# Taking the transposed queries from 16 rows of 128 tokens each, with an exp that reads PSUM in permuted order

## The chip, the cores and the metric

The kernel runs on one core of one Trainium2 chip. The core's engines work side by side and wait for each other through semaphores: PE (TensorE, the matmuls), DVE (VectorE), ACT (ScalarE), POOL (GpSimd) and SP (SyncE, which here only issues transfers). The metric is the device time of one execution in microseconds; lower is better. Profiles are of one execution, and in them "us" are counted from the first instruction.

## The reference

Two steps follow each other, in float32. First, attention with pooled keys: for each of four batches, 12288 queries `q` of 128 channels attend to 768 keys, which are 4 x 4 means of `kv` (384 x 32 positions) times a weight matrix; the values are the same as the keys. Then a mixture of adapters: each of the 49152 result rows picks two of eight experts, and a low-rank correction is added.

```
kv_pool = kv.reshape(B, H // r, r, W // r, r, C).mean(axis=(2, 4))      # r = 4
k = v = kv_pool.reshape(B, -1, C) @ w_sr
a = softmax(q @ k^T / sqrt(C));  x = (a @ v).reshape(B * S, D)
logits = x @ w_gate                         # 8 experts, top 2, weights by softmax of the two
out = x + sum over the two experts e of  w_e * ((x @ A[e]) @ B[e])
```

The output has 49152 rows of 128 floats.

## The kernel before, in words

The tokens are taken in 96 *chunks* of T = 512, and four chunks make a *group* of GT = 2048 (24 groups in all). In a group the kernel is free to choose which token stands in which column, as long as the exp's output, the attention rows and the stores agree.

**How queries reach PE.** PE needs q transposed, channels on partitions. For groups 0 and 1, `load_q` loads q in float32 and `turn_q` transposes it on PE in four parts, with a copy on ACT (L116). For groups 2 to 23, `cast_q` writes a bf16 copy to DRAM with a POOL-issued transfer, and `load_qT` (L84) reads it with one transposing DMA on SP's queue. Before the change that DMA reads the group as 128 rows of 16 tokens: row p, token j is token 16p + j of the group, and it lands in column 128j + p of `qT`. A chunk is a quarter of these columns. The transpose of a group is issued at the first chunk of the group before it; `qT` has four buffers.

**One chunk.** `scores` runs three times (r = 0, 1, 2). Each time PE writes two 128-key blocks of scores into a PSUM tile `sg` of 128 x 2 x 512 floats (two buffers), and ACT's exp (L246) turns the 1024 floats of each partition into fp16 `em`. Then `attend` takes 128-column pieces of `em`, one for each s = 0 to 3, as the stationary operand, so that partition p of the result `acc` belongs to column 128s + p of the chunk. `normalize`, `top`, `route`, `gates`, `transposes`, `down`, `gate` and `up` do the softmax division and the adapters on DVE, POOL, ACT and PE. `finish` (L363, L364) adds the correction on DVE and stores the chunk from SP: partition p holds four consecutive tokens, so each of the 128 runs is 2 KB. The output tiles `osb` have six buffers.

**The order of the work.** It is written out by hand: every call is wrapped in `keep`, which keeps program order on its engine. The main loop runs over chunks k, with the score matmuls of chunk k between the attend matmuls of an earlier one and the adapter work of still earlier ones. While a batch runs, the keys of the next batch are loaded (L96, on SP) and summed on POOL (L171).

**The start.** Before all that, the weights are loaded from ACT's queue, and on SP's queue come group 0's queries (L105, one transfer of 1 MB), 24 transfers of 256 KB with the first batch's `kv` (L98), and group 1's queries in four transfers. The first batch's keys are summed on DVE and PE, part by part as they land.

Of the kernel before, what the change touches and what calls it, by code (L numbers as in the profile page):

```python
# [14 lines left out]
AF = mybir.ActivationFunctionType  # L15
# [5 lines left out]
def kernel(  # L21
# [10 lines left out]
    nc = tc.nc  # L32
    P = 128
# [6 lines left out]
    S = T // P  # L40
    GC = 4
    GT = GC * T
# [4 lines left out]
    scale = 1.0 / float(np.sqrt(C))  # L47
# [17 lines left out]
    keep = tc.keep_in_program_order  # L65

    def mm(*a, **k):
        return keep(nc.tensor.matmul(*a, **k))  # L68
# [6 lines left out]
    q_bf, qT, kvr = {}, {}, {}  # L75
# [5 lines left out]

    def load_qT(g):
        t = qpool.tile([P, GT], BF16, tag="qT", name="qT")
        keep(nc.sync.dma_start(t.rearrange("c (j p) -> c j p", p=P),  # L84
                               q_bf[g].rearrange("(p j) c -> p (j c)", p=P), transpose=True))
        qT[g] = t


# [9 lines left out]
            keep(nc.sync.dma_start(kvr[b, h][:, r, x], src[:, :, x * 4 * C:(x + 1) * 4 * C]))  # L98


    def load_q(g, lo, hi):
        if g not in q_f:
            q_f[g] = xpool.tile([P, GT // P, C], FP32, tag="xn", name="qf")
        src = q[0, g * GT:(g + 1) * GT].rearrange("(p j) c -> p j c", p=P)
        keep(nc.sync.dma_start(q_f[g][:, lo:hi], src[:, lo:hi]))  # L105

    def turn_q(g, m, engine):
        if m == 0:
# [11 lines left out]
    q_f = {}  # L120
    w_sr_sb = const.tile([P, C], FP32)
    keep(nc.scalar.dma_start(w_sr_sb, w_sr))
    w_gate_sb = const.tile([P, E], FP32)
    keep(nc.scalar.dma_start(w_gate_sb, moe_w_gate))
    load_q(0, 0, GC * S)
    for h in range(3):
        for r in range(4):
            for x in range(2):
                load_kv(0, h, r, x)
    for m in range(GC):  # L130
        load_q(1, m * S, m * S + S)
# [102 lines left out]
    em, acc, xn, xg, srt, gw = {}, {}, {}, {}, {}, {}  # L234
# [3 lines left out]
    def scores(k, r):  # L238
        b = k // NB
        if r == 0:  # L240
            em[k] = ppool.tile([P, J, T], FP16, tag="em", name="em")
        rhs = qT[k // GC][:, (k % GC) * T:(k % GC + 1) * T]
        ps = ps_s.tile([P, 2, T], FP32, tag="sg", name="sg")
        for i in range(2):
            mm(ps[:, i], kfT[b][:, 2 * r + i], rhs, start=True, stop=True)
        keep(nc.scalar.activation(em[k][:, 2 * r:2 * r + 2], ps, AF.Exp, bias=0.0, scale=scale))  # L246

    def attend(k, s):
        b = k // NB
# [111 lines left out]
    def finish(k):  # L361
        osb = opool.tile([P, S, C], FP32, tag="osb", name="osb")
        keep(nc.vector.tensor_tensor(osb, dp[k], xn[k][:, :, 0:C], op=ALU.add))  # L363
        keep(nc.sync.dma_start(  # L364
            out[k // GC * GT:(k // GC + 1) * GT].rearrange("(p j) c -> p j c", p=P)
            [:, k % GC * S:(k % GC + 1) * S], osb))
        for d in (em, acc, xn, xT, hgT, hp, hg, dp):
            d.pop(k, None)

# [5 lines left out]
    for h in range(3):  # L375
        for item in sums[h]:
            item()
        rest[3 * h]()
        if h > 0:
            scores(2, h - 1)  # L380
        rest[3 * h + 1]()
        if h > 0:
            scores(3, h - 1)
            rest[3 * h - 1]()
        scores(0, h)
        scores(1, h)
# [35 lines left out]
    for k in range(LA, last + 3):  # L422
        b, i = divmod(k, NB)
# [3 lines left out]
        if k % GC == 0:  # L427
            g = k // GC
            if 2 <= g + 1 < B * NG:
                load_qT(g + 1)  # L430
            if 4 <= g + 2 < B * NG and g + 2 not in q_bf:
                cast_q(g + 2)
        if b + 1 < B:
            if i == 4:
                sums, rest = prepare(b + 1, nc.gpsimd)
            if 4 <= i < 16:
                h, j = divmod(i - 4, 4)
# [28 lines left out]
        for u_ in ku:  # L466
            up(u_)
            finish(u_)
# [25 lines left out]
        if not ks:  # L494
            for u_ in ku:
                up(u_)
                finish(u_)
            ku = []
        kh = kx
        if b + 1 < B and 8 <= i < 20:  # L500
            h, j = divmod(i - 8, 4)
# [33 lines left out]
```

The softmax here doesn't subtract the row's maximum and nothing guards it: scores larger than these inputs give would overflow.

## Time and profile before

| | |
|---|---|
| median of 9 runs | 426.51 us (425.78 to 426.8) |
| the profiled execution | 426.8 us, with a span of 424.8 us from its first to its last instruction |
| busy share of PE / DVE / ACT / POOL | 91% / 77% / 69% / 38% |
| exp, L246 | 288 instructions, 1023 ns each |
| transposing DMA, L84 | 22 on SP's queue, median 8.1 us from issue to landing |
| stores, L364 | 96 of 256 KB, median 3.3 us to landing |
| DMA packets | 71172, of them 49904 under 512 B |
| granted TensorE clock | 0.975 of full speed on average |

An engine's busy time is the sum of its instructions' durations. Rows of groups give the line, engine, operation, output <- input, the count, then busy time and mean of one, then the idle time of the engine just before them and who ended it. Rows of waits read "engine, line <- who was waited for: us in total, times, longest". Timeline rows give the start and the length in us; several instructions in a row on one engine are merged, with their count behind the x. "SPq" is SP's queue while it issues a transfer.

### The profile page before, as it was taken

Reading aid. Unit: us, or ns where it says so; the run is one execution under the profiler, and the core shown is the slowest. Engines: PE = TensorE matmul, PEld = TensorE weight load, DVE = VectorE, ACT = ScalarE, POOL = GpSimd, SP = SyncE. Lnnn points to the kernel's source line nnn. Section 1 sums busy time; section 2 is a strip of 40 time slices with the busy share of each in tenths; the row PEclk is TensorE's granted clock in tenths of the full one; section 3 lists DMA queues with packets and bytes.
Section 4 is the critical chain, followed back from the end, with each engine's and each line's share of the span. In section 5 each row is a group of like instructions: output and inputs, shape, how many; then the busy total and the mean of one; then the engine's idle time right before and its main releaser. Section 6 shows DMA issues by size and latency. Waiting matters only on the chain.

```text
span 424.8 us, 11322 instructions
## 1 busy us (share of the span) xinstructions
PE 385.7 (91%) x4515; PEld 309.9 (73%) x4589; DVE 327.4 (77%) x967; ACT 293.1 (69%) x336; POOL 162.5 (38%) x263
## 2 busy tenths in 40 slices
PE   3798899999999999999999999999999989999753
PEld 3566777777878877787888778777878877788642
DVE  2544778787988878779888878779888888888853
ACT  2488567676777777676787777676777866677522
POOL 0010357965320557964330467963231312222000
PEclk9999999999999999999999999999999999999955
DMA  8999567776556999895848999757584627332112
GB/s 301 367 241 260 124 178 191 292 152 150 125 125 131 332 213 269 311 162 124 148 122 151 315 276 254 262 143 148 128 171 129 150 76 174 113 113 76 51 60 90
DMA packets 71172, 76.43 MB, mean 180 GB/s; under 512 B 49904, under 2 KB 50160, under 8 KB 70640
## 3 DMA queue, kind: packets, MB, share of 16 engines
q1 hardware_dynamic: 70128, 64.11, 52.1%
q0 software_dynamic: 704, 11.54, 15.0%
q8 instruction: 36, 0.59, 0.6%
q14 instruction: 16, 0.13, 0.1%
q10 hardware_dynamic: 288, 0.07, 0.1%
HBM read 50.53 MB, written 36.70 MB: 205 GB/s over the span
## 4 chain that ended last, share of the span: by engine, by line
PE 68%; DVE 11%; POOL 10%; ACT 4%; issue 3%; DMA 2%; SPq 1%; ACTq 0%; DVEq 0%; POOLq 0%
PE acc L68 27%; PE sg L68 18%; PE tt_ps L68 9%; PE d_ps L68 5%; PE h_ps L68 5%; POOL kvr L171 4%; DVE hg L350 3%; ACT em L246 2%; DVE osb L363 2%; POOL over L293 2%; DVE xn L263 2%; PE v_ps L68 1%; SPq L98 1%; DMA w_sr_sb<-in_w_sr_dram 1%; DMA kvr<-in_kv_dram 1%
## 5 line engine op out<-in xcount | busy, mean ns | idle before, releaser
L246 ACT ACTIVATE em<-sg 128x1024 f16<-128x1024 f32 x288 | 280.7, 1023 | 97.1 <-PE sg L68 66.5
L68 PE MATMUL acc<-vx,em 128*128 128x137 f16 x2304 | 174.7, 225 | 2.0 <-DVE xn L263 1.9
L68 PE MATMUL sg<-qT,kfT 128*128 128x512 bf16 x502 | 154.9, 378 | 2.7 <-ACT em L246 2.2
L68 PEld LDWEIGHTS <-em 128*128 128x128 f16 x2304 | 150.4, 98 | 4.9 <-DVE xn L263 2.2
L68 PEld LDWEIGHTS <-tts 128*128 128x128 bf16 x768 | 59.2, 99 | 53.0 <-ACT tts L334 5.6
L350 DVE TENSOR_TENSOR hg<-h_ps,gw 128x512 bf16<-128x512 f32 x96 | 66.1, 689 | 30.5 <-POOL gw L315 17.9
L293 POOL TENSOR_TENSOR over<-xn,srt 128x128 f32<-128x128 f32 (+1 forms) x54 | 19.8, 384 | 175.3 <-DVE srt L281 175.3
L263 DVE TENSOR_TENSOR xn<-acc,rinv 128x544 f32<-128x544 f32 x96 | 69.6, 725 | 3.3
L171 POOL TENSOR_TENSOR kvr<-kvr 128x512 f32<-128x512 f32 x54 | 67.4, 1269 | 2.6 <-DMA kvr<-in_kv_dram 2.3
L363 DVE TENSOR_TENSOR osb<-d_ps,xn 128x512 f32<-128x512 f32 x96 | 66.0, 690 | 2.7 <-PE d_ps L68 2.6
L336 DVE COPY tts<-tt_ps 128x1024 bf16<-128x1024 bf16 (+1 forms) x95 | 63.9, 673 | 2.4 <-PE tt_ps L68 2.4
L68 PEld LDWEIGHTS <-xn 128*128 128x128 bf16 x384 | 29.5, 99 | 28.6 <-issue 6.1
L68 PEld LDWEIGHTS <-kfT 128*128 128x128 bf16 x576 | 45.9, 97 | 6.0 <-issue 3.7
L68 PE MATMUL tt_ps<-id_bf,xn 128*128 128x128 bf16 x384 | 37.6, 221 | 7.8 <-DVE hg L350 4.8
L68 PE MATMUL h_ps<-a_bf,tts 128*128 128x128 bf16 x384 | 37.8, 222 | 7.3 <-ACT tts L334 3.8
L258 DVE RECIPROCAL rinv<-acc 128x4 f32<-128x4 f32 x96 | 17.4, 181 | 32.8 <-PE acc L68 32.1
L68 PE MATMUL d_ps<-b_bf,tts 128*128 128x128 bf16 x384 | 38.0, 224 | 3.6 <-DVE hg L350 1.0
L68 PE MATMUL tt_ps<-id_bf,hg 128*128 128x128 bf16 x384 | 38.1, 223 | 3.2 <-DVE hg L350 2.8
L281 DVE MAX8 srt<-xn 128x8 f32<-128x8 f32 x384 | 34.6, 153 | 0.2
L68 PEld LDWEIGHTS <-hg 128*128 128x128 bf16 x384 | 26.1, 100 | 4.2 <-DVE hg L350 3.7
L312 ACT ACTIVATE th<-over 128x128 f32<-128x128 f32 (+2 forms) x33 | 9.1, 276 | 15.5 <-DVE over L298 12.2
L314 POOL TENSOR_TENSOR gw<-th,over 128x128 f32<-128x128 f32 (+1 forms) x27 | 11.0, 407 | 21.6 <-ACT th L312 21.5
(49 smaller groups left out, 163.3 us busy)
## 6 DMA issues: line engine op xcount, KB each, us to landing
out_dram<-osb SPq DMA_DIRECT2D x96, 256.0 KB, 3.3
kvr<-in_kv_dram SPq DMA_DIRECT2D x36, 512.0 KB, 6.3
qbf<-in_q_dram POOLq DMA_DIRECT2D x22, 512.0 KB, 7.0
kvr<-in_kv_dram SPq DMA_DIRECT2D x24, 256.0 KB, 5.2
qf<-in_q_dram SPq DMA_DIRECT2D x1, 1024.0 KB, 5.1
qf<-in_q_dram SPq DMA_DIRECT2D x4, 256.0 KB, 5.2
qT<-qbf SPq DMA_TRANSPOSE x22, 8.1
w_sr_sb<-in_w_sr_dram ACTq DMA_DIRECT2D x1, 64.0 KB, 5.3
```

Of the source, the lines that this page charges most:

```text
L68: return keep(nc.tensor.matmul(*a, **k))
L171: keep(adder.tensor_tensor(u[:, lo:hi], u[:, lo:hi], v[:, lo:hi], op=ALU.add))
L246: keep(nc.scalar.activation(em[k][:, 2 * r:2 * r + 2], ps, AF.Exp, bias=0.0, scale=scale))
L258: keep(nc.vector.reciprocal(ri, acc[k][:, :, VC]))
L263: keep(nc.vector.tensor_tensor(x, acc[k][:, :, 0:VC], ri.unsqueeze(2).broadcast_to([P, S, VC]), op=ALU.mult))
L281: keep(nc.vector.max(srt[k0][:, m, s], xn[k][:, s, C:VC]))
L293: keep(eng.tensor_tensor(d, lg, so[:, :, i].unsqueeze(2).broadcast_to([P, n, 8]), op=ALU.subtract))
L312: keep(nc.scalar.activation(th, arg, AF.Tanh, bias=0.0, scale=0.5))
L314: keep(eng.tensor_tensor(w[:, 0:n], th, mask, op=ALU.mult))
L336: keep(nc.vector.tensor_copy(sb[:, lo:hi], ps[:, lo:hi]))
L350: keep(nc.vector.tensor_tensor(hg[k].rearrange("p s (e r) -> p (s e) r", e=E), hp[k].rearrange("p s (e r) -> p (s e) r", e=E), gw[k0][:, m ...
L363: keep(nc.vector.tensor_tensor(osb, dp[k], xn[k][:, :, 0:C], op=ALU.add))
```

## The change

The change renumbers the tokens inside a group.

- The transposing DMA of groups 2 to 23 reads the group as 16 rows of 128 tokens. Row r, token j is token 128r + j, and it lands in column 16j + r. It is still one instruction a group.
- In these groups, a chunk m has the 32 values of j from 32m on. With j written as (j, s), 8 x 4, its 512 columns lie in the order (j, s, r) in PSUM. The exp reads them as (s, r, j), so that its output is again cut into four pieces s of 128 columns, and partition (r, j) holds the tokens 128r + 32m + 4j + s. `em` is written in one contiguous run as before.
- The store of a chunk goes to rows (r, j) of the output, 16 x 8 runs of four tokens, 2 KB each.
- Groups 0 and 1, which PE transposes, load their queries in the same numbering; their exps are not edited. `load_q` now issues one transfer for each chunk, so group 0's single transfer of 1 MB becomes four of 256 KB.

```diff
     def load_qT(g):
         t = qpool.tile([P, GT], BF16, tag="qT", name="qT")
-        keep(nc.sync.dma_start(t.rearrange("c (j p) -> c j p", p=P),
-                               q_bf[g].rearrange("(p j) c -> p (j c)", p=P), transpose=True))
+        keep(nc.sync.dma_start(t.rearrange("c (j r) -> c j r", r=16),
+                               q_bf[g].rearrange("(r j) c -> r (j c)", r=16), transpose=True))
         qT[g] = t
...
+    def rows_of(tokens):
+        return tokens.rearrange("(r m j s) c -> m r j (s c)", r=16, m=GC, s=S)
+
     def load_q(g, lo, hi):
...
-        src = q[0, g * GT:(g + 1) * GT].rearrange("(p j) c -> p j c", p=P)
-        keep(nc.sync.dma_start(q_f[g][:, lo:hi], src[:, lo:hi]))
+        src = rows_of(q[0, g * GT:(g + 1) * GT])
+        for m in range(lo // S, hi // S):
+            keep(nc.sync.dma_start(
+                q_f[g][:, m * S:(m + 1) * S].rearrange("p s c -> p (s c)"), src[m]))
...
-        keep(nc.scalar.activation(em[k][:, 2 * r:2 * r + 2], ps, AF.Exp, bias=0.0, scale=scale))
+        o = em[k][:, 2 * r:2 * r + 2]
+        if k // GC > 1:
+            ps = ps.rearrange("p i (j s r) -> p i s r j", s=S, r=16)
+            o = o.rearrange("p i (s r j) -> p i s r j", s=S, r=16)
+        keep(nc.scalar.activation(o, ps, AF.Exp, bias=0.0, scale=scale))
...
         keep(nc.sync.dma_start(
-            out[k // GC * GT:(k // GC + 1) * GT].rearrange("(p j) c -> p j c", p=P)
-            [:, k % GC * S:(k % GC + 1) * S], osb))
+            rows_of(out[k // GC * GT:(k // GC + 1) * GT])[k % GC],
+            osb.rearrange("p s c -> p (s c)")))
```

## The prediction

> **What bounds the kernel now.** I read the page's busy times and its line of costliest groups first, then the waits, then a timeline of one undisturbed stretch, and last the first 20 us, because the change also touches the loads there.
>
> ```profile
> PE 385.7 (91%) x4515; PEld 309.9 (73%) x4589; DVE 327.4 (77%) x967; ACT 293.1 (69%) x336; POOL 162.5 (38%) x263
> ...
> L246 ACT ACTIVATE em<-sg 128x1024 f16<-128x1024 f32 x288 | 280.7, 1023 | 97.1 <-PE sg L68 66.5
> ...
> L84 SPq DMA_TRANSPOSE qT<-qbf x22: 2055/3063/6147, 31.4 to 369.3; - x22
> ...
> ACT em L246 <- PE sg L68: 66.5, 77, 3.8
> ...
> PE sg L68 <- ACT em L246: 2.2, 6, 0.8
> ```
>
> PE is busy 91% of the span. ACT waits 66.5 us in all for PE's score matmuls, and PE waits 2.2 us for ACT's exps: PE sets the pace and ACT follows. The transposes that the change rewrites occupy SP's queue alone. In the middle of the kernel:
>
> ```profile
> 230.27 0.59 PE L68 MATMUL sg<-qT,kfT 128*128 128x512 bf16 x2
> ...
> 231.15 0.59 PE L68 MATMUL sg<-qT,kfT 128*128 128x512 bf16 x2
> ...
> 232.18 0.38 PE L68 MATMUL sg<-qT,kfT 128*128 128x512 bf16 x1
> ...
> 233.95 0.59 PE L68 MATMUL sg<-qT,kfT 128*128 128x512 bf16 x2
> ...
> 230.96 2.87 ACT L246 ACTIVATE em<-sg 128x1024 f16<-128x1024 f32 x3 [0.81 <-PE sg L68]
> ...
> 225.80 4.73 SPq L84 DMA_TRANSPOSE qT<-qbf  x1
> ...
> 240.53 6.01 SPq L84 DMA_TRANSPOSE qT<-qbf  x1
> ```
>
> A chunk takes 233.95 - 230.27 = 3.68 us, a group of four 240.53 - 225.80 = 14.73 us. ACT needs 2.87 us of each chunk for three exps (0.925 us apart, since they overlap) and then idles 0.81 us for PE.
>
> The start is another regime, loads:
>
> ```profile
> 0.74 0.39 SPq L105 DMA_DIRECT2D qf<-in_q_dram  x1
> 1.18 17.01 SPq L98 DMA_DIRECT2D kvr<-in_kv_dram  x24
> ...
> 11.75 5.24 DMA kvr<-in_kv_dram
> ...
> SPq L98 <- DMA w_sr_sb<-in_w_sr_dram: 1.4, 1, 1.4
> ```
>
> The chain that ended last passes through a kv load that is issued at 11.75 and lands at 16.99, so a late load there moves everything. DMA share by windows is 0.96 to 1.05 from 4 to 24 us, at 337 to 406 GB/s.
>
> **The exp (L246), the decisive term.** Chunks 8 to 95, 264 of the 288 exps, will read PSUM with an inner step of 64 floats (256 B) in runs of 8 instead of one run of 1024. Count, elements and output stay. The cost per element is in the trace: the 128x512 cast of L116 from PSUM takes 586 ns (median), the 128x1024 exp 1023, so (1023 - 586)/512 = 0.85 ns per element. No ACT row of the trace reads PSUM with a step. The bounds for an exp are therefore 0, and one more pass, 1024 x 0.85 = 0.87 us[...]; a gain is excluded, since the contiguous read is already the simplest pattern.
>
> [...] the second matmul of a pair adds 0.59 - 0.38 = 0.21 us for 512 columns, so PE writes 512/0.21 = 2.4 floats per ns and partition[...]. [...] I take 0, near the unstrided row of the same instruction, and keep 0.87 for the range.
>
> How much could be hidden? The two sg buffers decide it. The third score pair, at 232.18, writes the buffer of the first, whose exp runs from 230.96 to about 231.95. That leaves 0.23 us per exp; beyond it PE waits, with the down-projection, the rest of attend and the next chunk queued behind it. [...] the exp would be 0.925 + 0.87 = 1.80 us and ACT the bound: 264 x 1.80 + 5 us of tanh = 480 us for a stretch that lasts from about 51 to 401 = 350 us, so +130 us; by the row, 0.
>
> **The transposes (L84).** 22 instructions stay 22. [...] The read of one row becomes contiguous over 32 KB. SP's issue takes 2.06 to 6.15 us now and landing 4.7 to 11.3 us. A group's transpose is issued one group ahead. In the trace the last of its 256-byte packets ends 8.3 to 25 us before the first exp of that group, so it would have to take 8.3 us longer to stop PE. Stores and kv loads behind it on SP have cover too: between 225.80 and 240.53 SP is occupied 4.73 us by the transpose and under 5 us by eight other issues, and osb has six buffers, 22 us of chunks. Below, the transpose may get several us shorter; nothing waits for it, so that gains nothing. Value 0 either way.
>
> **The stores (L364) and casts.** 96 stores stay 96, in 2 KB runs; only the rows' order changes. DVE's osb waits 2.6 us in all, and for PE alone. 0. The POOL casts are unedited. PE and DVE issue the same instructions in the same order.
>
> **The first loads (L105).** Group 0's query load goes from one transfer of 1024 KB (8 KB runs) to four of 256 KB (2 KB runs): three more issues ahead of all 24 kv loads. At 0.39 us each, or 0.6 like the kv issues, that is 1.2 to 1.8 us on SP. Then there is a second effect. [...] six SP transfers start freely. Now these are the 1 MB query and five kv loads, and the sixth waits for w_sr, 1.4 us, until 6.0. After, they are four quarters and two kv loads, and the third kv load waits for w_sr. From there kv issues follow 0.645 us apart. If w_sr still lands at 6.0, kv load n comes at 6.0 + 0.645(n - 3) instead of 6.0 + 0.645(n - 6): 1.9 us later. The transfers absorb part of that, because 1.6 MB instead of 2.3 MB is queued at 6.0, at some 390 GB/s, and runs out near 6.6, while a new issue needs more than a microsecond to move bytes: a hole of some 0.7 us, so +0.7 to +1.9.
>
> But w_sr should land sooner. Between 3 and 4 us the DMA view counts 50 packets on SP's queue and 48 on ACT's: the queues alternate packet by packet. w_sr's 128 packets of 512 B, 8 per engine, each wait behind an 8 KB packet, 0.33 us per round (16 engines, 48 rounds per us). Behind 2 KB packets, by bytes, a round takes 0.33 x 2.5/8.5 = 0.10 us, so w_sr ends about 1.9 us sooner and lands near 4.3. Then the issue of kv load n is 4.3 - 6.0 + 3 x 0.645 = 0.2 us later, with no hole. Value +0.3 us, bounds -0.5 (turn_q also starts sooner, and its first quarter lands first) and +1.9.
>
> **The sum.** 426.8 us, the profiled execution (424.8 span, 2.0 around it), + 0 + 0 + 0 + 0.3 = 427.1. That execution is 0.3 above the median of the nine runs, so 426.8 in the median's terms. 0.2% is 0.85 us, about what a measurement of this kernel can tell from no change: the band is 425.7 to 427.4.
>
> **The rivals.**
>
> 1. ACT becomes the bound (slower). Place: L246. Price: 0.87 us per exp; 426.8 + 130 = 557 us. It decides from 0.23 us per exp upward, a 22% longer exp. Partial penalties lie between: 0.43 us costs 0.43 - 0.23 = 0.20 us on 88 chunks, +18 us (445); 0.5 us makes it about +30 us (457). [...] Against: PE's write rate.
>
> 2. The start loses its loads (slightly slower): w_sr lands at 6.0 as before, or the four quarters delay the kv loads otherwise. 427.5 to 428.7 us. For: the chain runs through a kv load. Against: the alternation of packets.
>
> 3. The transposes get slow enough to be waited for: 16 rows 32 KB apart instead of 4 KB. From 8.3 us more each; at 10 us more about 22 x 1.7 = 37 us, 464. For: the DMA share is 1.00 from 226 to 240.7. [...]
>
> 4. Faster: earlier query quarters and a lighter DMA shift the start by -0.9 us or more, 425.5. For: turn_q stands on PE from 7.40. Against: the kv bytes still have to land.
>
> **How the numbers follow.** All hidden, within 0.2%: 0.44. Start slower by more (rival 2): 0.14. Partial ACT penalty: 0.10. Full one: 0.17. Slow transposes: 0.03. Faster: 0.12. So faster 0.12, same 0.44, slower 0.44. The likeliest is 426.8, with 425.9 to 428.5 of its own. The range runs from 425.4 to 465: it takes in the partial penalties and the slow transposes and leaves out the full penalty and a little below.
>
> **What would show it.** The mean of the em row: 1023 to 1050 ns is my case, 1250 the point where PE begins to wait ("PE sg <- ACT em" far above 2.2 us), about 1900 rival 1, with ACT's busy share over 90%. The issue of the third kv load: near 4.3 (mine) or 6.0 (rival 2), and the kv landing on the chain at 17.0 + 0.3 or + 1 and more. A PE or ACT wait on DMA qT would be rival 3. I would be wrong outright if the em row stayed at 1023 and the middle groups still left 14.7 us.

## The result: slower by 0.85%, most of it lost in the first 30 us

The changed kernel takes 430.18 us in the median of 9 runs (428.8 to 430.86), the kernel before 426.38 beside it. The ratio is 1.0085, with a 95% interval of 1.0076 to 1.0095. The profiled execution took 428.8 us, the fastest of them, with a span of 426.9 us; a second profile, further down, is of a longer one.

First the lines of the changed kernel that answer to those of the prediction: busy times and the exp from the page, the transposes, the two waits between PE and ACT, and a stretch in the middle.

```profile
PE 387.3 (91%) x4515; PEld 310.3 (73%) x4589; DVE 327.1 (77%) x967; ACT 293.1 (69%) x336; POOL 162.4 (38%) x263
...
L255 ACT ACTIVATE em<-sg 128x1024 f16<-128x1024 f32 x288 | 280.7, 1023 | 101.0 <-PE sg L68 71.3
...
L84 SPq DMA_TRANSPOSE qT<-qbf x22: 2612/3194/6072, 33.5 to 371.5; - x22
...
ACT em L255 <- PE sg L68: 71.3, 77, 8.7
...
PE sg L68 <- ACT em L255: 2.2, 6, 0.8
```

The exp is still 1023 ns, although 264 of the 288 now read PSUM in steps of 256 B. PE waits for ACT 2.2 us, as before. ACT's longest wait for PE has grown from 3.8 to 8.7 us, and it is a single one: the first exp.

```profile
233.02 2.87 ACT L255 ACTIVATE em<-sg 128x1024 f16<-128x1024 f32 x3 [0.81 <-PE sg L68]
...
228.07 5.11 SPq L84 DMA_TRANSPOSE qT<-qbf  x1
...
242.79 6.07 SPq L84 DMA_TRANSPOSE qT<-qbf  x1
```

A group still takes 242.79 - 228.07 = 14.72 us and three exps 2.87. From the trace, the first exp of chunk 8 comes 2.1 us later than before (53.47 for 51.37), and the last exp of the kernel 2.05 us later (402.01 for 399.96). Between them lie 348.54 us, and 348.59 before: nothing is lost or won. The transposes did change: the page of the changed kernel counts few small packets where the one before counted 49904, since each transpose now moves as 16 packets of 32 KB.

```profile
DMA packets 26900, 76.43 MB, mean 179 GB/s; under 512 B 4896, under 2 KB 5152, under 8 KB 26144
```

This does nothing for the time. SP's issue stayed near 3.1 us (3.06 and 3.19), landing went from 8.1 to 7.9 us in the median, and nobody waits for either.

One thing behind the last exp did change. The kernel ends 1.0 to 1.3 us after its last store has landed, and that store, now 16 x 8 runs, takes 2.8 us to land where it took 2.0. The first line is of the kernel before, the second of the changed one:

```profile
out_dram<-osb SPq DMA_DIRECT2D x1, 256.0 KB, 2.0
...
out_dram<-osb SPq DMA_DIRECT2D x1, 256.0 KB, 2.8
```

In this profile it does not show in the sum, because the half clock near the end, of which more below, began later behind the last exp (6.5 us for 3.8), and from the last exp to the last `osb` (the last output tile on DVE) it took 0.6 us less.

So most of the loss sits in the start. SP's queue and PE there, then windows of the changed kernel (length; PE busy and its matmuls; the same for weight loads, DVE, ACT and POOL; granted clock, DMA share, GB/s):

```profile
0.74 2.61 SPq L109 DMA_DIRECT2D qf<-in_q_dram  x4
3.39 15.55 SPq L98 DMA_DIRECT2D kvr<-in_kv_dram  x24
...
5.14 4.14 PE L68 MATMUL qT_ps<-id_f,qf 128*128 128x128 f32 x16
10.57 1.18 PE L68 MATMUL kpT_ps<-id_f,kvr 128*128 128x128 f32 x8 [1.29 <-DVE kvr L180]
13.22 1.97 PE L68 MATMUL kpT_ps<-id_f,kvr 128*128 128x128 f32 x8 [1.47 <-DVE kvr L180]
15.79 1.19 PE L68 MATMUL kfT_ps<-kpT,w_sr_sb 128*128 128x256 f32 x2 [0.61 <-DVE kpT L205]
17.50 1.89 PE L68 MATMUL sg<-qT,kfT 128*128 128x512 bf16 x4 [0.52 <-DVE kfT L212]
...
4.00:6.00 2.00, 1.28 (x6) 1.31 (x7) 0.17 (x1) 0.00 (x0) 0.00 (x0) 1.00 1.08 252
...
12.00:14.00 2.00, 0.78 (x4) 0.79 (x5) 1.34 (x2) 0.00 (x0) 0.00 (x0) 0.65 1.05 405
14.00:16.00 2.00, 1.39 (x7) 1.02 (x6) 0.42 (x1) 0.00 (x0) 0.00 (x0) 0.50 1.06 407
16.00:18.00 2.00, 1.48 (x4) 0.49 (x5) 0.98 (x3) 0.00 (x0) 0.00 (x0) 0.50 1.05 403
18.00:20.00 2.00, 2.00 (x11) 1.25 (x10) 1.85 (x4) 1.43 (x2) 0.00 (x0) 0.65 1.05 406
```

Two things are new. From 4 to 6 us the DMA engines are full (share 1.08) but move 252 GB/s, where the kernel before moved 365. And from 12.6 to 19.4 us PE's granted clock is half. In the kernel before the windows show 1.00:

```profile
4.00:6.00 2.00, 0.00 (x0) 0.00 (x0) 0.00 (x0) 0.00 (x0) 0.00 (x0) 1.00 0.96 365
...
10.00:12.00 2.00, 2.00 (x15) 1.76 (x14) 0.94 (x2) 1.17 (x2) 0.00 (x0) 1.00 1.02 352
12.00:14.00 2.00, 1.39 (x11) 1.03 (x10) 0.88 (x2) 0.00 (x0) 0.00 (x0) 1.00 1.04 361
```

A caution on the 1.00: the trace's clock records begin at 9.2 us in the changed kernel and at 11.2 us in the kernel before, and a window ahead of the first record shows 1.00 without one. Ahead of it PE runs at half speed in both: in the kernel before, the transposes of q start 213 ns apart, and those of the keys, of the same size, 109 ns apart from 11.2 us on; the changed kernel has 213 ns for the former up to 8.9 us. (The average of 0.975 in the table counts these first 11.2 us as full.) So both kernels begin at half clock and rise from it. What is new is that the changed one falls back.

The late loads make the first four key sums on DVE end at 13.81 us instead of 12.45, +1.36. The two holes of PE behind them, 1.29 and 1.47 us, are followed by the half clock: the four score matmuls take 1.89 us instead of 1.04, the two of kfT 1.19 instead of 0.67, and the first exp starts at 18.57 instead of 15.60. Of these 2.97 us, 0.87 are made up before chunk 8.

### The profile page after: what moved, and what is told of

Its sections match the earlier page's. It is cut to its first block, busy times and chain, and to the rows that moved or that the text cites. A ratio compares the mean times of both kernels' runs of the same rounds, so it can differ in the third digit from the quotient of the medians.

```text
span 426.9 us, 11328 instructions
## 1 busy us (share of the span) xinstructions
PE 387.3 (91%) x4515; PEld 310.3 (73%) x4589; DVE 327.1 (77%) x967; ACT 293.1 (69%) x336; POOL 162.4 (38%) x263
## 4 chain that ended last, share of the span: by engine, by line
PE 69%; DVE 11%; POOL 10%; ACT 4%; issue 3%; SPq 1%; DMA 1%; ACTq 0%; DVEq 0%; POOLq 0%
PE acc L68 27%; PE sg L68 19%; PE tt_ps L68 9%; PE d_ps L68 5%; PE h_ps L68 5%; POOL kvr L176 4%; DVE hg L359 3%; ACT em L255 2%; DVE osb L372 2%; PE kpT_ps L68 2%; POOL over L302 2%; DVE xn L272 2%; PE v_ps L68 1%; DMA kvr<-in_kv_dram 1%; DVE tts L345 1%
## 5 line engine op out<-in xcount | busy, mean ns | idle before, releaser
L255 ACT ACTIVATE em<-sg 128x1024 f16<-128x1024 f32 x288 | 280.7, 1023 | 101.0 <-PE sg L68 71.3
```

The source lines that it names most:

```text
L255: keep(nc.scalar.activation(o, ps, AF.Exp, bias=0.0, scale=scale))
```

## The experiments

**Which part of the change.** Two kernels halve the change: one keeps the new body and the old start, one the reverse. Old start: in the changed kernel,

```diff
     def load_q(g, lo, hi):
-        src = rows_of(...)        # four transfers of 16 x 8 runs
+        src = q[0, g * GT:(g + 1) * GT].rearrange("(p j) c -> p j c", p=P)
+        keep(nc.sync.dma_start(q_f[g][:, lo:hi], src[:, lo:hi]))
...
     def finish(k):               # stores of chunks 0 to 7 in the old numbering too
```

> The changed kernel, but groups 0 and 1 keep the old numbering in their query loads (one of 1 MB, four of 256 KB) and in their stores; groups 2 to 23 have the new transposes, exps and stores. Theory A: the start is all of the cost, so 426.4 us within 0.6, with the first exp near 15.6 us as before. Rival C: in executions without a profile the new transposes, exps or stores cost 1 to 2 us as well (the changed kernel's profiled execution is 2.0 us longer, its median 3.8 us): 428 to 430 us.

Measured: 426.94 us, ratio 1.0015 (1.0008 to 1.0021), the first exp at 15.37 us. The new transposes, permuted exps and stores of groups 2 to 23 leave 0.15% (at most 0.21%). Its trace says where: from chunk 8's first exp to the last exp it takes 348.56 us, as before, and the last store lands 2.8 us after its issue.

New start alone, the same edit the other way round in the kernel before:

> The kernel before, but groups 0 and 1 take the new numbering in their query loads (eight transfers of 256 KB) and in their stores; groups 2 to 23 are as before. Theory A: 430.2 us (428.8 to 430.9 in single executions), PE clock at half speed for some microseconds from about 12 us on. Rival C: 428 us or less.

Measured: 429.37 us, ratio 1.0063 (1.0045 to 1.0081), the first exp at 18.50 us and half clock from 12.5 to 19.4. That is 0.8 us under the 430.2 expected, but most of the loss comes with the start. For rival C, a cost in the body, 0.3 to 0.6 us are left, and the traces of all fourteen profiled executions put it at the very end: between chunk 8's first exp and the last exp all take 348.5 to 348.7 us. The last store lands after 2.8 us in the seven whose last chunks are stored in the new numbering and after 2.0 in the other seven, and the time from the last `osb` to the end is 3.9 to 4.1 us in the former and 3.1 to 3.3 in the latter. No kernel changes the last store alone.

**Number of transfers, or the way they are cut.** In the kernel before, the single load of 1 MB is only divided:

```diff
-    load_q(0, 0, GC * S)
+    for m in range(GC):
+        load_q(0, m * S, m * S + S)
```

> The kernel before with one edit: group 0's query load is four transfers of 256 KB in the old numbering (128 rows, 2 KB runs at 8 KB pitch). Theory A: what costs is the order in which the query loads read DRAM (16 rows at 64 KB pitch), which moves 250 GB/s instead of about 390 in the first microseconds; the number of transfers is harmless. Then this is 426.4 us within 0.6 (or a little under, since w_sr lands sooner), and 2 to 8 us shows over 350 GB/s. Rival B: three more issues ahead of the kv loads[...] cost it. Then 428.5 to 430 us, as in the changed kernel.

Measured: 426.92 us, ratio 1.0018 (1.0003 to 1.0034), but in two clusters: 13 executions from 425.92 to 427.33, like the kernel before, and 9 from 428.36 to 429.21. (The expectation of a later run has them as 14 and 8.) The mean granted clock parts them too: 0.971 to 0.982 in the lower, 0.967 to 0.969 in the upper. The profiled one, 428.77, belongs to the upper one. Its windows:

```profile
4.00:6.00 2.00, 1.00 (x4) 0.73 (x5) 0.65 (x3) 0.00 (x0) 0.00 (x0) 1.00 0.96 342
6.00:8.00 2.00, 2.00 (x11) 1.78 (x11) 0.17 (x1) 0.71 (x2) 0.00 (x0) 1.00 1.05 400
...
10.00:12.00 2.00, 0.70 (x7) 0.46 (x5) 0.00 (x0) 0.26 (x1) 0.00 (x0) 1.00 0.94 336
12.00:14.00 2.00, 1.21 (x7) 0.98 (x8) 1.34 (x2) 0.00 (x0) 0.00 (x0) 0.80 1.05 375
14.00:16.00 2.00, 1.39 (x5) 0.65 (x3) 0.42 (x1) 0.00 (x0) 0.00 (x0) 0.50 1.02 381
```

The loads run at nearly the old rate here (342 and 400 GB/s, where the kernel before moved 365 and 382), yet the clock falls. PE has finished turning the queries sooner (at 9.63 instead of 11.14 us), since the weights have landed sooner (at 4.5 instead of 6.0), and then stands idle between 10 and 12 us (0.70 us busy) before the key sums arrive. In the kernel before, the late weights kept PE busy (2.00) in just this window. So the first theory, that only slow loads cost, was too simple; the rival, that the number of transfers costs in itself, does not fit the lower cluster. The clock became a theory of its own.

**The clock.** Eleven matmuls that nobody reads fill PE's holes, 5 ahead of the first key transposes and 6 in the middle of them:

```diff
             for n, (r, i, c) in enumerate(parts):
+                if (b, h) == (0, 0) and n % 8 == 0:
+                    warm_pe(5 + n // 8, <an acc tile in PSUM>, 0)   # id_bf x qT, 512 columns
                 mm(ps[:, i], kvr[b, h][:, r, i, c * C:(c + 1) * C], id_f, is_transpose=True,
```

In the changed kernel:

> The changed kernel with eleven extra matmuls of 512 columns on PE (5 before and 6 within the first key transposes, into a PSUM tile nobody reads yet), so that PE is not idle while the first kv loads are late. Theory A2: the changed start costs twice: the 64 KB pitch makes the first key sums some 1.3 us late (12.45 to 13.81), and PE's hole then halves the granted clock for 6.8 us, which costs another 1.5 to 2.5 us. Then the clock stays at 1.0 until 26 us and the time is 427.3 to 428.3 us instead of 430.2. Rival D: the clock is a by-product without weight, the late loads are all of it: 429.5 to 430.5.

Measured: 428.18 us, ratio 1.0035 (1.0023 to 1.0047). The loads are as slow as before, the clock stays up:

```profile
4.00:6.00 2.00, 1.35 (x7) 1.38 (x8) 0.17 (x1) 0.00 (x0) 0.00 (x0) 1.00 1.14 263
...
12.00:14.00 2.00, 2.00 (x12) 0.94 (x11) 1.34 (x2) 0.00 (x0) 0.00 (x0) 1.00 1.04 388
14.00:16.00 2.00, 1.13 (x6) 0.52 (x5) 0.65 (x2) 0.00 (x0) 0.00 (x0) 1.00 1.07 403
```

That splits the 0.85%: about 0.5% is the clock (430.18 - 428.18 = 2.0 us) and 0.35% is there without it. Its trace, 1.57 us longer than that of the kernel before, has the 0.35% in two pieces. The last kv load of the batch lands at 24.19 us instead of 22.78, and the last key sum waits for it:

```profile
18.50 5.69 DMA kvr<-in_kv_dram
...
24.28 0.69 DVE L185 TENSOR_TENSOR kvr<-kvr 128x512 f32<-128x512 f32 x1 [0.27 <-DMA kvr<-in_kv_dram]
```

That makes chunk 8's first exp 0.88 us late, and the last exp 1.00. The other 0.57 us lie behind the last `osb`, in the last store. The control is the split kernel with the same eleven matmuls:

> The kernel before with group 0's load split in four, old numbering, and the same eleven extra matmuls. The split kernel without them came out in two clusters, 14 executions at 425.9 to 427.3 and 8 at 428.4 to 429.2, its profile with halved clock from 12 to 20 us. Theory A2: the upper cluster is the halved clock and goes away: all executions at 425.8 to 427. Rival D: both clusters stay.

Measured: 426.44 us, ratio 1.0002 (0.9992 to 1.0011). 13 of 14 executions lie from 425.89 to 427.29 and one at 428.39. The upper cluster is gone: the mean clock of the one at 428.39, 0.976, is not that of the upper cluster. The extra matmuls themselves cost nothing. In its trace the first four key sums end 0.7 us late (13.17) and chunk 8 begins only 0.1 us late (51.47), so this much lateness of the first sums costs next to nothing by itself.

Then the changed kernel once more, for a profile of a typical execution:

> The changed kernel once more, unedited, for a second profile: the first one, 428.8 us, is the fastest of its executions, most are near 430.3. Theory A2: an execution near 430 has the same first key sums, but the clock is halved at another moment, or for longer than 6.8 us, in the start or at the end; the groups 2 to 23 keep their lengths. Rival C: the groups in the middle are longer.

It took 431.16 us. The first key sums and the first exp (18.55) come at the times of the first profile, but the clock is half until after 22 us:

```profile
14.00:16.00 2.00, 1.39 (x7) 1.02 (x6) 0.43 (x1) 0.00 (x0) 0.00 (x0) 0.50 1.06 402
...
18.00:20.00 2.00, 2.00 (x8) 1.25 (x7) 1.83 (x4) 1.45 (x2) 0.00 (x0) 0.50 1.05 405
20.00:22.00 2.00, 2.00 (x12) 2.00 (x11) 0.00 (x0) 0.49 (x1) 0.00 (x0) 0.50 1.06 408
```

In the trace's clock records the half clock lasts 6.83 us in the first profile and 10.24 in this one, two and three times 3.41. Chunk 8's first exp is then 3.65 us late instead of 2.1, the last exp 3.74, and the last store adds 0.6 (3.9 us from the last `osb` to the end, for 3.3). Ahead of its fall in the first profile PE was not idle: from 9.17 to 12.59 us it was busy for 1.28 us of 3.41.

The traces of the two kernels show more of this. Their clock records last 3.41 us or whole multiples of it (6.83, 389.12 and 392.53 us), but for the last one, which runs past the end of the span. Continued in steps of 3.41 us, they cut each span into windows. Of the 230 whole windows at full clock, three are followed by half clock, and in these PE was busy, as the profile counts it, for 1.28, 1.30 and 1.45 us; the other 227 all have 1.91 us or more. The way back took more: the three windows at half clock that are followed by full clock, two of them ahead of the first record, have 2.89, 3.33 and 3.41 us, and those that are followed by half clock 2.31 us or less. What happens between these values the two traces do not show. The first record begins at 11.20 us in the kernel before and at 9.17 in the changed one, 2.03 us apart and so not at the same place in a window. The same hole may then fall into one window or be shared between two, which would fit a program that loses its clock in some executions and not in others; that this is the reason was not shown.

**Why the loads are slow.** The first idea was the addresses in DRAM, 16 row blocks 64 KB apart. In the changed kernel, group 0's quarters become contiguous blocks of 256 KB (row blocks 16 KB apart) and group 1's have row blocks 32 KB apart:

```diff
+        if g == 0:
+            return tokens.rearrange("(m p s) c -> m p (s c)", m=GC, s=S)
+        if g == 1:
+            v = tokens.rearrange("(h r m j s) c -> h m r j (s c)", h=2, r=16, m=2, s=S)
...
```

> The changed kernel with two other numberings for the first two groups. Group 0: each quarter is one contiguous block of 256 KB, so the 16 row blocks of a quarter lie 16 KB apart instead of 64 KB, with the same 2 KB runs and the same four transfers. Group 1: 16 rows 32 KB apart. Theory A with the pitch as the cause: group 0's load runs at 350 GB/s or more between 3 and 6 us, the total is 426.4 us within 0.8, and group 1's load (22 to 25 us) lies between 250 and 390 GB/s. If instead the cause is that 16 KB of each quarter are contiguous per row block, whatever the pitch, group 0 stays near 250 GB/s and the total near 430.

Measured: 429.38 us, ratio 1.007 (1.0057 to 1.0083). Group 0's load was fast, group 1's slow:

```profile
4.00:6.00 2.00, 1.46 (x6) 1.19 (x7) 0.66 (x4) 0.00 (x0) 0.00 (x0) 1.00 1.04 384
...
10.00:12.00 2.00, 0.46 (x4) 0.22 (x3) 0.36 (x1) 0.00 (x0) 0.00 (x0) 1.00 1.03 374
12.00:14.00 2.00, 1.61 (x8) 1.50 (x8) 0.95 (x2) 0.00 (x0) 0.00 (x0) 0.63 1.02 377
...
22.00:24.00 2.00, 1.78 (x11) 0.96 (x9) 1.56 (x5) 1.81 (x3) 0.00 (x0) 1.00 1.06 259
```

The time was still 3 us over, not the 426.4 us expected, because PE was nearly idle between 10 and 12 us (busy for 0.46 us) and lost its clock, as in the split kernel. And the pitch (the distance between the blocks) was not yet shown as the cause: a contiguous quarter is a single row of 128 runs, while every slow load is cut as 16 x 8 runs. The last run separates the two. It is the kernel before with its queries loaded in quarters that read other addresses in the 16 x 8 form:

```diff
-        src = q[0, g * GT:(g + 1) * GT].rearrange("(p j) c -> p j c", p=P)
...
+        if g == 0:   # blocks 72 KB apart, runs 8 KB apart
+            src = q[0, 0:16 * 144].rearrange("(r x) c -> r x c", r=16)[:, 0:128]
+            src = src.rearrange("r (j m s) c -> m r j (s c)", m=GC, s=S)[m]
+        else:        # blocks 18 KB apart, runs side by side
+            src = q[0, GT + m * 576:GT + (m + 1) * 576].rearrange("(r x) c -> r x c", r=16)[:, 0:32]
+            src = src.rearrange("r (j s) c -> r j (s c)", s=S)
...
```

> The kernel before with eight query loads of 256 KB that read other addresses: group 0's as 16 blocks of 8 runs of 2 KB, runs 8 KB apart as in the old numbering, blocks 72 KB apart; group 1's with runs side by side, blocks 18 KB apart. Both are cut as 16 x 8 runs and not as 128, as in the changed kernel, but neither has 16 KB blocks at 32 or 64 KB pitch. Groups 0 and 1 so compute with other rows of q. Theory P (the DRAM addresses, 16 row blocks 32 or 64 KB apart, are slow): both at 350 GB/s or more, from 3 to 6 us and in the last 2 us of group 1's loads. Theory F (the transfer's form, 16 x 8 instead of 128 runs, is slow, whatever the addresses): both at about 250 GB/s, as in the changed kernel.

Measured: 429.59 us in one run, 426.69 for the kernel before beside it. Its windows at group 0's and group 1's loads, and its first score matmuls:

```profile
3.00:5.00 2.00, 0.57 (x4) 0.50 (x4) 0.29 (x1) 0.12 (x1) 0.00 (x0) 1.00 0.90 261
...
23.00:25.00 2.00, 1.78 (x11) 1.09 (x10) 1.18 (x4) 1.81 (x3) 0.00 (x0) 1.00 1.04 272
...
17.56 1.89 PE L68 MATMUL sg<-qT,kfT 128*128 128x512 bf16 x4 [0.52 <-DVE kfT L214]
```

Both loads are slow (the split kernel moves 310 and 396 GB/s from 3 to 5 and from 22 to 24 us), at addresses that differ from the changed kernel's and from each other. Theory P falls: it is the form, 16 blocks of 8 runs, and not the pitch. What in the form makes it slow is not shown; the kv loads, cut as 32 x 4 runs, move 403 to 407 GB/s from 12 to 20 us in the changed kernel. The time fits the account of the clock: the clock records begin only at 21.2 us here, so the 1.00 ahead of them says nothing, and the score matmuls at 17.56 us take 1.89 us, as at half clock in the changed kernel (1.04 in the kernel before). In this execution PE still ran at half speed there.

**The tail, and a faster kernel.** The clock also falls in the kernel before, from 403.7 us to its end. First the split kernel got the extra matmuls at the start, and 4 more around the adapter transposes of the tail:

```diff
         for x_, h_ in pairs[:1]:
+            if k > NCHUNK:
+                warm_pe(4, <an sg tile in PSUM>, NCHUNK // GC - 1)
             transposes(x_, h_, not ks)
+            if not ks:
+                warm_pe(4, <an sg tile in PSUM>, NCHUNK // GC - 1)
```

> The split kernel with the extra matmuls at the start, and with 4 more around each group of adapter transposes after the last chunk's scores, where the profile before shows the clock at 0.5 from about 404 us on. If the halved clock in the tail lengthens the chain there, 424.5 to 425.8 us; if the extra matmuls stand in the way of the real ones, or the tail is set by DVE and ACT, 426.3 to 428.

Measured: 425.48 us, ratio 0.9957 (0.9934 to 0.998). Its trace still shows 6.8 us of half clock in the tail, so the next kernels start the extra matmuls one chunk earlier and add 4 behind the second transposes of an iteration. On the kernel before:

> The kernel before with extra matmuls on PE in its tail alone (4 of 512 columns around each group of adapter transposes after the last scores, into PSUM tiles that nobody reads): its start has no halved clock, its tail has one from about 404 us. Theory A2 (a hole on PE costs the clock, and the clock costs time where PE is on the chain): 424 to 425.5 us. Rival D (the clock is without weight): 426.4 or more.

Measured: 424.26 us, ratio 0.9948 (0.9932 to 0.9963), faster than both kernels. Two windows of its tail, after the two of the kernel before:

```profile
405.00:408.00 3.00, 2.29 (x21) 2.29 (x22) 1.49 (x3) 0.66 (x1) 0.00 (x0) 0.50 0.23 87
408.00:411.00 3.00, 1.90 (x19) 1.63 (x17) 0.01 (x1) 1.01 (x1) 0.00 (x0) 0.50 0.00 0
...
405.00:408.00 3.00, 2.39 (x33) 2.10 (x34) 1.40 (x3) 0.94 (x2) 0.00 (x0) 1.00 0.26 93
408.00:411.00 3.00, 2.20 (x19) 1.02 (x16) 1.88 (x4) 0.63 (x1) 0.00 (x0) 1.00 0.01 3
```

With the clock held up in the tail, the new body can be weighed better. The same tail on the old-start kernel:

> The same tail on the changed kernel with the old numbering in groups 0 and 1, so it differs from tail_before in the transposes, the permuted exps and the stores of groups 2 to 23 alone. Theory A: these are worth nothing, so it is within 0.4 us of tail_before. Rival C: the 0.15% that the old-head kernel lay above the kernel before is theirs; then 0.5 to 0.9 us above tail_before.

Measured: 424.58 us, ratio 0.9958 (0.9944 to 0.9971), 0.3 us above tail_before, with intervals that overlap. In the two traces chunk 8's first exp to the last exp takes 348.57 and 348.58 us and the last exp to the last `osb` 19.10 and 19.11. From there to the end it is 4.1 and 3.3 us, which is the last store again.

And the changed kernel with contiguous quarters in groups 0 and 1 and extra matmuls at both ends:

> The changed kernel, but with groups 0 and 1 numbered so that each quarter of their queries is one contiguous block of 256 KB (four transfers each, row blocks 16 KB apart), and with the extra matmuls at both ends. Theory A2: with the pitch and the clock both mended nothing is left of the loss: within 0.6 us of tail_before, group 0's and group 1's loads both at 350 GB/s or more. If separate transfers or the new numbering cost by themselves: 426 us or more.

Measured: 424.77 us, ratio 0.996 (0.9947 to 0.9972), 0.5 us above tail_before; the loads move 349 to 383 GB/s from 4 to 8 us and 402 from 22 to 24. With the form of the query loads and the clock mended, some 0.5 us of the loss remain, and the last store, with 3.9 us from the last `osb` to the end for 3.3, is about as much.

## Why the prediction was right and wrong

The likeliest case, all hidden, did not happen. What happened is rival 2, a start that loses its loads, at more than its price. The measured 430.18 us lies inside the stated range of 425.4 to 465 by luck: the range was that wide for penalties on the exp and the transposes, which cost nothing, while the interval of the likeliest case (425.9 to 428.5) and the price of rival 2 (427.5 to 428.7) both end below it.

- *The exp.* Right. The decisive term was put at 0 and is 0: 1023 ns. The upper bound, one more pass, would have given 1.8 us and 557 us in all; it was an estimate. A step of 256 B costs ACT nothing here. Whether PE's write rate (2.4 floats per ns and partition in the kernel before) has to do with it no run tests.
- *Transposes and casts.* Right that nothing waits for them. It was not foreseen that the packets would change from 256 B to 32 KB (2048 to 16 a transpose), but nobody waits there.
- *The stores.* Put at 0 because DVE does not wait for them. The end of the kernel waits for the last one, and in the new form it lands 0.8 us later. That is most or all of what the new body costs.
- *The first loads.* This term failed: +0.3 with an upper bound of +1.9, and the new start alone measured +2.75 (429.37 - 426.62). Three parts of it were off. The quarters take 0.60 us each to issue, the upper of the two values named, so the third kv load is issued at 4.68 and not 4.3. The transfers were taken to run at some 390 GB/s whatever their form, and the quarters run at 250 to 290. (The first packet of the query load moves 1.0 us after its issue in the kernel before and 1.5 us after it in the changed one.) The eighth kv load, the one that the first key sums wait for, was issued 0.85 us later than before (8.07 for 7.22), where 0.2 was forecast, and landed 1.36 later (13.02 for 11.66). And nothing in the sum had PE's clock in it, which is 2.0 of the 3.8 us.
- *w_sr.* Predicted to land near 4.3 behind 2 KB packets. In the split kernel, which has such packets in the old form, it landed at 4.5; in the changed kernel at 2.5, and why the form brings it forward by that much more is not shown. That the third kv load would wait for it was an estimate from the one such wait of the kernel before (the sixth kv load's, 1.4 us); it did not wait. But the sign of what follows was wrong: PE's transposes of q moved forward (they end at 9.28 for 11.14), into a time when nothing follows them, and left the hole in which the clock falls.
- *What it was to look like.* The kv landing on the chain: the changed kernel's first exp, not 0.3 but 3 us late.

## What to carry to other kernels

Look at the granted clock in the start and the tail as well as in the middle, and do not trust a 1.00 ahead of the first clock record: there the distance between equal matmuls tells the clock (213 ns at half, 109 at full for the transposes here). Where PE was busy for 1.28 to 1.45 us of 3.41, half clock followed: the first key sums came 1.36 us late, and the half clock behind that cost another 2.0 us; in the split kernel the weights came 1.5 us early and opened such a hole too. Eleven matmuls that nobody reads were a cheap cure, worth 0.5% at the start, and those in the tail another 0.5%. Permuting ACT's read from PSUM in steps of 256 B was free (1023 ns), but keep the form of a DMA as plain as it was, because the number and length of its runs did not tell its speed (252 GB/s as 16 x 8 runs of 2 KB, 342 as one row of 128). And look at the last store by itself: nothing after it hides its landing, 2.8 us here for 2.0.

## What the hardware showed that was not expected

- The half clock in the start came in stretches of 6.83 and 10.24 us, in the changed kernel after a window of 3.41 us in which PE was busy for 1.28 us and not idle (in the traces of the two kernels the windows ahead of a fall have 1.28 to 1.45 us, the others at full clock 1.91 or more); the same program falls in some executions and not in others (9 of 22 of the split kernel, by their times).
- A load of 128 runs of 2 KB moves 340 to 400 GB/s as one row of 128 runs (342 and 396 in the split kernel) and about 400 as 32 x 4, and 240 to 290 as 16 x 8, with the engines' busy share at 0.9 to 1.1 in all. A packet of 2 KB takes 139 ns on average from 4 to 6 us in the changed kernel and 86 in the kernel before, where they are those of kv.
- A store of 256 KB with nothing beside it lands after 2.8 us as 16 x 8 runs and after 2.0 us as 128 runs.
- A transpose of 16 rows of 32 KB moves in 16 packets of 32 KB, where 128 rows of 4 KB moved in 2048 of 256 B; time to landing stayed the same (7.9 for 8.1 us).
